# Capped attention before two expert layers: values in tiles of 32 columns in one piece with the sums, and the first two pairs' loads ahead of all others

## The chip, the cores and the metric

The kernel runs on one core of a Trainium2 chip. The core has a matrix engine (PE, whose weight loads the profile lists as PEld), three engines for element-wise work (DVE, ACT, POOL), and SP, which here issues nearly all DMAs. Each engine works through its own instructions in a fixed order and waits for the others by semaphores. The metric is the device time of one execution in microseconds (us), median of several.

## The reference

```
scores = q @ k.T / sqrt(64)                      # 2 x 12 heads, 448 x 448
scores = cap * tanh(scores / cap)                # cap = 30
attn = exp(scores - max); attn = attn / (sum(attn) + 1e-9)
x = attn @ v                                     # -> 896 tokens x 768
xn = x / rms(x) * rms_g
y = (silu(xn @ w_gate) * (xn @ w_val)) @ w_out   # 768 -> 1536 -> 768
a, b = y @ w1, y @ w2
out = ((a * b) @ w3) @ w_out2                    # 768 -> 1024 -> 1024 -> 768
```

All is float32. The maximum is not subtracted: tanh bounds the scores. The last two products have no nonlinearity between them, so the kernel multiplies w3 by w_out2 ahead, beside the attention.

## The kernel before

**Attention.** The 24 heads lie in 12 pairs, two heads to a pair, and two pairs make what is called a set here (`d` in the code, six sets). A set has seven groups of key chunks: six groups hold 128 keys of both heads of one pair, the two pairs taking turns, and the seventh holds the last 64 keys of all four heads. For a group `g`, `scores` (L406) multiplies on PE into a PSUM bank of ring `s`, which holds two groups; `tanh` (L425) and `exp` (L432) run over it on ACT and leave it in SBUF; `pv` (L438) multiplies by the values into `po`, 64 columns of the matrix for each head; and for every two groups `total` (L453) multiplies by ones into `pn`, 32 columns for each of the four heads, which gives the sums of the softmax. In this text S0 is the scores block of group 0, V0 its values block, N the sums of two groups. A float32 matmul shows as two passes, so a block of two matmuls is four rows (x4), and one of four is x8. When a set is through, its values are copied out (`take`), its sums inverted on DVE (`invert`, L486), spread by eight DMAs (`spread`, L497) and multiplied in (L505); squares are added up, and when the first or last six pairs are through, `normalize_x` makes the root mean square, scales (L322) and splits x into a high and a low half.

**Beside it.** `last_product` (L619) multiplies w3 by w_out2 in 64 items of three matmuls (L654 to L656), whose weights are unpacked by POOL, ACT and DVE (`weights`, L243). The items fill PE while the last set is inverted and normalised; then the first experts' products (L824 to L826) begin.

**Order.** All work is added to a planner (`Plan`, L55) as tasks with an engine, an estimated length and a rank. `order` (L89) plays the tasks through with these estimates, the ready task of lowest rank first, and the engines' instructions stand in the order that comes out. A task is one block on PE: scores, values and sums are tasks of their own (L541 to L553). Load tasks carry a rank that says how early SP issues them (`load_head` L387, `load_val` L402). The load of `cap` (L1115) is issued before the planner's work; it sets `tsc`, the scale that tanh reads.

Of the kernel before, what the change touches and what calls it, by code (L numbers as in the profile page):

```python
# [19 lines left out]
P = 128  # L20
B, H, S, D = 2, 12, 448, 64
# [5 lines left out]
CD = DM // P  # L27
# [4 lines left out]
KP = NK * P  # L32
NG = HP * 7 // 2
CQ = S // 4
CW = P // 4
# [19 lines left out]
class Plan:  # L55
# [19 lines left out]
    def add(self, engines, run, rank, after=(), makes=(), uses=(), size=0, behind=()):  # L75
        if not isinstance(engines, dict):
            engines = {engines[0]: engines[1]}
        i = len(self.tasks)
        for m in makes:
            self.bufs[m["tag"]].append((rank if m["first"] is None else m["first"], i, m))  # L80
        held = list(makes) + [u for u in uses if u is not None]
        for h in held:
            h["users"] += 1
        self.tasks.append(
            dict(on=engines, run=run, rank=rank, after=[x for x in after if x is not None], makes=list(makes), held=held, size=size, behind=list(behind))
        )
        return i
# [81 lines left out]
def body(ctx: ExitStack, tc, qk, v, cap, wgv, wdn, rg, w12, w3t, wo2, out):  # L169
# [44 lines left out]
    def layer(es, bounded):  # L214
# [145 lines left out]
        def attend():  # L360
# [26 lines left out]
            def load_head(p):  # L387
                def run(e, cols, new):
                    if new:
                        heads[p] = ring(ap, "qk", [P, S + KP])  # L390
                    e.dma_start(out=heads[p][:, cols], in_=qk[p][:, cols])

                when = first_of(p) - (7 if p == 0 else 5)
                cuts = [slice(0, S + P), slice(S + P, S + KP)] if p == 0 else [slice(0, S + KP)]
                h_done[p] = []
                for n, c in enumerate(cuts):
                    h_done[p].append(
                        add(("SP", 0.45), lambda e, c=c, n=n: run(e, c, n == 0), when + 0.1 * n, behind=h_done[p], makes=[] if n else [qkb[p]], uses=[qkb[p]] if n else [],
                            size=P * (c.stop - c.start) * 4)
                    )  # L400

            def load_val(p):  # L402
                def run(e):
                    vals[p] = ring(ap, "v", [P, 7, D])
                    e.dma_start(out=vals[p], in_=v[p])

                v_done[p] = add(("SP", 0.45), run, first_of(p) - 5.5 if p else -6.85, makes=[vb[p]], size=P * 7 * D * 4)

            def scores(g):
                def run(e):  # L410
                    chunks[g] = ring(ps, "s", [P, 2, 512], name="pss")
                    use = parts(g)
                    for j in range(2):
                        for p, c in use:

                            q = heads[p][j * D : (j + 1) * D]
                            if c < 3:
                                at, to, ks = j, slice(0, P), slice(S + c * P, S + (c + 1) * P)
                            else:
                                at, to, ks = p % 2, across(p, j), slice(S + 3 * P + j * D, S + 3 * P + (j + 1) * D)  # L420
                            e.matmul(chunks[g][to, at, :S], q[:, ks], q[:, :S], start=True, stop=True)  # L421

                return run

            def tanh(g):  # L425
                def run(e):
                    s = chunks[g]
                    chunks[g] = ring(ap, "t", [P, 2, S])
                    e.activation(chunks[g], s[:, :, :S], AF.Tanh, scale=tsc)  # L429

                return run

            def exp(g):
                def run(e):
                    e.activation(chunks[g], chunks[g], AF.Exp, scale=acap)  # L435

                return run

            def pv(g):


                def run(e):
                    for i in range(2):
                        for p, c in parts(g):
                            if c == 0 and i == 0:
                                pos[p] = ring(ps, "o", [P, 512], name="po")
                            rows, n = (slice(0, P), i) if c < 3 else (across(p, i), p % 2)
                            w = vals[p][rows, 2 * c + i if c < 3 else 6, :]
                            e.matmul(pos[p][i * D : (i + 1) * D, :S], w, chunks[g][rows, n, :], start=c == 0, stop=c == 3)  # L449

                return run

# [75 lines left out]
            for p in range(NP):  # L528
                load_head(p)
                load_val(p)  # L530
            exps, x_alloc, sq_last, pv_last, sum_last = {}, {}, {}, {}, {}
            every = []
            for g in range(NG):
                use = parts(g)
                sb = buf("s")
                qs = [qkb[p] for p, _ in use]
                need = []
                for p, c in use:
                    need += h_done[p][:1] if p == 0 and c == 0 else h_done[p]
                a = add(("PE", 0.83), scores(g), g - 2, after=need, makes=[sb], uses=qs)  # L540
                a = add(("ACT", 1.02), tanh(g), g, after=[a], makes=[tb[g]], uses=[sb])  # L541
                exps[g] = a = add(("ACT", 1.06), exp(g), g + 0.1, after=[a], uses=[tb[g]])
                c, last = use[0][1], use[-1][1] == 3
                a = add(("PE", 0.83), pv(g), g + 1, after=[exps[g]] + [v_done[p] for p, _ in use] + [pv_last.get(p) for p, _ in use],
                        makes=[ob[p] for p, c in use if c == 0], uses=[tb[g]] + [vb[p] for p, _ in use] + [ob[p] for p, c in use if c])
                for p, _ in use:
                    pv_last[p] = a
                if use[-1][0] % 2 == 0:
                    continue
                d = g // 7  # L550
                from_ = [g] if last else [g - 1, g]
                t = add(("PE", 0.83), total(d, c), g + 1.2, after=[exps[x] for x in from_] + [sum_last.get(d)], makes=[] if c else [nb[d]],
                        uses=[tb[x] for x in from_] + ([nb[d]] if c else []))  # L553
                sum_last[d] = t
                if not last:
                    continue
                r = g + 1.5
                b = 2 * d // (H // 2)
                taken = {}
                got = add(("DVE", 0.64), take_sum(d), r - 2, after=[t], makes=[smb[d]], uses=[nb[d]])  # L560
                for p in (2 * d, 2 * d + 1):
                    new = b not in x_alloc
                    taken[p] = add(dict(ACT=0.55, DVE=0.64), take(p), r - 2 + 0.1 * (p % 2), after=[a] + ([] if new else [x_alloc[b]]),
                                   makes=[xb[b]] if new else [], uses=[ob[p]] + ([] if new else [xb[b]]))
                    x_alloc.setdefault(b, taken[p])
                inv = [add(("DVE", 1.52), invert(d, c), r + 0.1 * c, after=[got], uses=[smb[d]]) for c in range(2)]
                for p in (2 * d, 2 * d + 1):
                    h = p % (H // 2)
                    sent = []
                    for i in range(4):  # L570
                        sent.append(add(("SP", 0.45), spread(p, i), r - 50, after=inv, behind=sent[-1:], makes=[] if i else [rbb[p]], uses=[smb[d]] + ([rbb[p]] if i else []), size=CW * S * 4))
                    a = add(("DVE", 0.66), normalize(p), r + 0.3, after=sent + [taken[p]], uses=[rbb[p], xb[b]])
                    every.append(a)
                    a = add(dict(DVE=0.66, POOL=1.3), square(p), r + 0.4, after=[a], makes=[sqb[p]] if h else [], uses=[xb[b]])
                    if h:
                        a = add(dict(DVE=0.66) if h == 5 else dict(DVE=0.66, POOL=1.3), add_square(p), r + 0.5, after=[a, sq_last[b]], uses=[sqb[p]])
                    sq_last[b] = a
                    every.append(a)
                    if p == NP // 2 + 1:
                        normalize_x(0, [sq_last[0]], g + 0.9)  # L580
# [531 lines left out]
                        add(("SP", 0.45), store(*done[1:]), -50, after=[done[0]], uses=[tmp[done[1]]], size=P * S * 4)  # L1112

        if bounded:
            nc.sync.dma_start(out=tsc, in_=cap.to_broadcast([P, 1]))  # L1115
            load_const()
            add(("SP", 0.45), lambda e: e.dma_start(out=rgt, in_=rg), -6.7, size=P * CD * 4)
            stored = last_product()
            over = attend()
        else:  # L1120
            attend_any()
            stored, over = [], []
# [62 lines left out]
```

## Time and profile before

| | |
|---|---|
| median of 3 runs | 624.87 us (624.56 to 625.26) |
| the profiled execution | 625.47 us, its span 623.3 us |
| PE busy | 608.6 us, 98% of the span |
| ACT, DVE, POOL busy | 265.7, 401.0, 141.6 us |
| attention on PE, first scores to last sums | 5.10 to 114.57 us |
| the first expert product | 145.68 us |

The span runs from the first to the last instruction of the profiled execution. The chain that ended last, 91% of it PE, says what each step waited for. A busy PE may still lose time: where the shape of the tiles in the matrix changes from one block to the next, a block takes longer, and this shows in how long the block stands in the chain, not as idle time.

### The profile page before, as it was taken

What the parts mean: (1) busy time and instruction counts of PE and PEld (TensorE: products, weight loads), DVE (VectorE), ACT (ScalarE), POOL (GpSimd) and SP (SyncE); (2) the same over time, 40 slices, a digit from 0 to 9 for tenths busy, and PEclk for the clock granted to TensorE, in tenths of its full rate; (3) what the DMA queues carried; (4) which work ended last, traced back from release to release, by engine and by line L of the source; (5) the groups of instructions that cost most, each with busy time, mean ns of one, the idle gap of its engine ahead of it and who ended that gap; (6) DMA issues with size and microseconds to landing.
All of it is one profiled execution on the core that took longest, in us unless ns stands there. A gap on an engine that the chain in (4) does not pass through costs nothing.

```text
span 623.3 us, 8065 instructions
## 1 busy us (share of the span) xinstructions
PE 608.6 (98%) x3088; PEld 490.6 (79%) x3088; DVE 401.0 (64%) x527; ACT 265.7 (43%) x359; POOL 141.6 (23%) x138
## 2 busy tenths in 40 slices
PE   5999999999999999999999999999999999999996
PEld 1222232798899999999999999999999999999995
DVE  2788685589866888435776555576657575627753
ACT  4988999156444343222334333333323343213220
POOL 3573200122343344211132222211122121000000
PEclk9999999999999999999999999999999999999999
DMA  8556421176455454218962323333331423105111
GB/s 309 214 177 209 148 60 42 54 238 203 146 197 167 169 193 148 68 67 255 331 217 102 101 102 103 102 110 121 119 108 50 152 90 97 35 0 151 56 49 64
DMA packets 32063, 82.93 MB, mean 133 GB/s; under 512 B 3728, under 2 KB 20752, under 8 KB 32016
## 3 DMA queue, kind: packets, MB, share of 16 engines
q1 hardware_dynamic: 32016, 82.33, 40.0%
q8 instruction: 26, 0.43, 0.3%
q14 instruction: 21, 0.17, 0.1%
HBM read 70.52 MB, written 9.04 MB: 128 GB/s over the span
## 4 chain that ended last, share of the span: by engine, by line
PE 91%; DMA 3%; DVE 2%; ACT 2%; issue 1%; SPq 0%; DVEq 0%; ACTq 0%
PE bank L826 22%; PE bank L825 22%; PE bank L824 22%; PE bank L1048 8%; PE pss L421 6%; PE po L449 6%; PE pn L463 3%; DMA wraw<-in_wgv 2%; DMA m_half<-mo 1%; DMA qk<-in_qk 1%; DVE whl L191 1%; DVE xraw L322 0%; ACT xn L184 0%; DVE sm L486 0%; ACT t L435 0%
## 5 line engine op out<-in xcount | busy, mean ns | idle before, releaser
L191 DVE TENSOR_TENSOR whl<-wraw,whl 128x768 fp32r<-128x768 f32 (+1 forms) x86 | 74.5, 867 | 69.5 <-POOL whl L188 58.5
L268 POOL TENSOR_SCALAR wraw<-wraw 128x768 int32<-128x768 uint32 (+1 forms) x68 | 76.0, 1118 | 152.9 <-DMA wraw<-in_w 57.8
L826 PE MATMUL bank<-xn,whl 128*128 128x448 f32 x288 | 105.8, 367 | 0.8 <-DVE whl L191 0.8
L824 PE MATMUL bank<-xn,whl 128*128 128x448 f32 x288 | 105.7, 367 | 0.3 <-ACT mo L184 0.3
L825 PE MATMUL bank<-xn,whl 128*128 128x448 f32 x288 | 105.6, 367 | 0.0
L272 DVE SCALAR_TENSOR_TENSOR wraw<-wraw 128x768 int32<-128x768 int32 (+1 forms) x76 | 71.4, 939 | 47.1 <-POOL wraw L268 47.1
L276 DVE SCALAR_TENSOR_TENSOR wraw<-wraw 128x768 int32<-128x768 int32 (+1 forms) x76 | 76.6, 1008 | 1.7
L188 POOL TENSOR_SCALAR whl<-wraw 128x768 fp32r<-128x768 f32 (+1 forms) x34 | 32.1, 943 | 196.4 <-PE bank L826 119.4
L184 ACT ACTIVATE whl<-wraw 128x768 fp32r<-128x768 f32 (+1 forms) x52 | 41.6, 801 | 73.8 <-PE bank L826 28.2
L824 PE MATMUL bank<-y,whl 128*128 128x448 f32 x192 | 70.7, 368 | 0.0
L825 PE MATMUL bank<-y,whl 128*128 128x448 f32 x192 | 70.7, 368 | 0.0
L826 PE MATMUL bank<-y,whl 128*128 128x448 f32 x192 | 70.7, 368 | 0.0
L259 ACT ACTIVATE wraw<-wraw 128x768 f32<-128x768 f32 (+1 forms) x54 | 47.5, 882 | 45.4 <-DMA wraw<-in_wgv 17.3
L826 PEld LDWEIGHTS bank<-xn,whl 128*128 128x128 f32 x288 | 54.1, 188 | 6.3 <-DVE whl L191 1.6
L824 PEld LDWEIGHTS bank<-xn,whl 128*128 128x128 f32 x288 | 54.1, 188 | 5.5 <-ACT mo L184 0.6
L825 PEld LDWEIGHTS bank<-xn,whl 128*128 128x128 f32 x288 | 54.1, 188 | 4.9
L824 PE MATMUL bank<-u,whl 128*128 128x448 f32 x144 | 52.8, 367 | 0.0
L826 PE MATMUL bank<-u,whl 128*128 128x448 f32 x144 | 52.8, 367 | 0.0
L825 PE MATMUL bank<-u,whl 128*128 128x448 f32 x144 | 52.8, 367 | 0.0
L421 PE MATMUL pss<-qk 64*128 64x448 f32 (+1 forms) x192 | 44.5, 604 | 5.1 <-DMA qk<-in_qk 5.1
L429 ACT ACTIVATE t<-pss,small 128x896 f32<-128x896 f32 x42 | 41.9, 998 | 10.7 <-PE pss L421 10.7
L435 ACT ACTIVATE t<-t,small 128x896 f32<-128x896 f32 x42 | 43.9, 1044 | 1.3
(99 smaller groups left out, 920.7 us busy)
## 6 DMA issues: line engine op xcount, KB each, us to landing
wraw<-in_wgv SPq DMA_DIRECT2D x24, 768.0 KB, 5.4
wraw<-in_w SPq DMA_DIRECT2D x16, 768.0 KB, 4.3
wraw<-in_wdn SPq DMA_DIRECT2D x12, 768.0 KB, 4.3
wraw<-in_w3t SPq DMA_DIRECT2D x16, 512.0 KB, 3.9
wraw<-in_wo SPq DMA_DIRECT2D x8, 768.0 KB, 6.6
qk<-in_qk SPq DMA_DIRECT2D x11, 480.0 KB, 4.5
m_half<-mo SPq DMA_DIRECT2D x16, 192.0 KB, 3.0
mo<-m_half SPq DMA_DIRECT2D x16, 192.0 KB, 5.1
```

Of the source, the lines that this page charges most:

```text
L191: e.tensor_tensor(lo, raw, r32(hi), op=ALU.subtract)
L259: e.activation(h, h, AF.Copy, scale=2.0**-112)
L268: e.tensor_scalar(l, l.bitcast(U32), 0.876 * 2.0**-29, 0.49, op0=ALU.mult, op1=ALU.add)
L272: e.scalar_tensor_tensor(l, h, 3, l, op0=ALU.logical_shift_left, op1=ALU.bitwise_or)
L276: e.scalar_tensor_tensor(l, h, -(2**31), l, op0=ALU.bitwise_and, op1=ALU.bitwise_or)
L421: e.matmul(chunks[g][to, at, :S], q[:, ks], q[:, :S], start=True, stop=True)
L429: e.activation(chunks[g], s[:, :, :S], AF.Tanh, scale=tsc)
L435: e.activation(chunks[g], chunks[g], AF.Exp, scale=acap)
L824: e.matmul(dst, whi[:, c, :], src(0, g, b), start=(g == 0), stop=False)
L825: e.matmul(dst, whi[:, c, :], src(1, g, b), start=False, stop=False)
L826: e.matmul(dst, wlo[:, c, :], src(0, g, b), start=False, stop=(g == total - 1))
L1048: e.matmul(st["bank", name], w[:, q, :], z_at(op, q, y), start=q == 0 and n == 0, stop=q == NQ - 1 and n == 2)
```

## The change

Values are multiplied in pieces of 32 columns (`CW`), the shape that the sums have, two matmuls for each head where one was. The values of two groups and their sums are one task on PE (`all_values`), which waits for both groups' exp; for the seventh group it is its values and sums. Scores could be put in one task by two (`two`), but the code has this off (`False and`). The queries and first 128 keys of the first two pairs are loaded first, then values and the other keys of both; `cap` is issued by ACT; `rg`, which is read at the end of attention, is issued later.

```diff
-                when = first_of(p) - (7 if p == 0 else 5)
-                cuts = [slice(0, S + P), slice(S + P, S + KP)] if p == 0 else [slice(0, S + KP)]
+                cuts = [slice(0, S + P), slice(S + P, S + KP)] if p < 2 else [slice(0, S + KP)]
+                whens = [(-8, -6.8), (-7.9, -6.7)][p] if p < 2 else [first_of(p) - 5]
...
-                v_done[p] = add(("SP", 0.45), run, first_of(p) - 5.5 if p else -6.85, makes=[vb[p]], size=P * 7 * D * 4)
+                v_done[p] = add(("SP", 0.45), run, first_of(p) - 5.5 if p > 1 else -6.85 + 0.1 * p, makes=[vb[p]], size=P * 7 * D * 4)
...
-                            w = vals[p][rows, 2 * c + i if c < 3 else 6, :]
-                            e.matmul(pos[p][i * D : (i + 1) * D, :S], w, chunks[g][rows, n, :], start=c == 0, stop=c == 3)
+                            for at in range(i * D, (i + 1) * D, CW):
+                                w = vals[p][rows, 2 * c + i if c < 3 else 6, at - i * D : at - i * D + CW]
+                                e.matmul(pos[p][at : at + CW, :S], w, chunks[g][rows, n, :], start=c == 0, stop=c == 3)
...
-                a = add(("PE", 0.83), scores(g), g - 2, after=need, makes=[sb], uses=qs)
-                a = add(("ACT", 1.02), tanh(g), g, after=[a], makes=[tb[g]], uses=[sb])
-                exps[g] = a = add(("ACT", 1.06), exp(g), g + 0.1, after=[a], uses=[tb[g]])
-                c, last = use[0][1], use[-1][1] == 3
-                a = add(("PE", 0.83), pv(g), g + 1, after=[exps[g]] + [v_done[p] for p, _ in use] + [pv_last.get(p) for p, _ in use],
-                        makes=[ob[p] for p, c in use if c == 0], uses=[tb[g]] + [vb[p] for p, _ in use] + [ob[p] for p, c in use if c])
...
+                two = False and use[0][1] < 3 and g > 1
+                if not two or use[0][0] % 2:
+                    of = [g - 1, g] if two else [g]
...
+                    a = add(("PE", 0.95 * len(of) - 0.18 * two), all_scores, of[0] - 2, after=[n for x in of for n in s_need[x][0]], makes=[s_need[x][1] for x in of], uses=[q for x in of for q in s_need[x][2]])
...
-                d = g // 7
-                from_ = [g] if last else [g - 1, g]
-                t = add(("PE", 0.83), total(d, c), g + 1.2, after=[exps[x] for x in from_] + [sum_last.get(d)], makes=[] if c else [nb[d]],
-                        uses=[tb[x] for x in from_] + ([nb[d]] if c else []))
-                sum_last[d] = t
+                c, last, d = use[0][1], use[-1][1] == 3, g // 7
+                of = [g] if last else [g - 1, g]
+
+                def all_values(e, of=of, d=d, c=c):
+                    for x in of:
+                        pv(x)(e)
+                    total(d, c)(e)
+
+                pair = (2 * d, 2 * d + 1)
+                banks_ = [ob[p] for p in pair] + [nb[d]]
+                a = add(("PE", 1.67 if last else 2.45), all_values, of[0] + 1, after=[exps[x] for x in of] + [v_done[p] for p in pair] + [sum_last.get(d)],
+                        makes=[] if c else banks_, uses=[tb[x] for x in of] + [vb[p] for p in pair] + (banks_ if c else []))
+                sum_last[d] = t = a
...
-            nc.sync.dma_start(out=tsc, in_=cap.to_broadcast([P, 1]))
+            nc.scalar.dma_start(out=tsc, in_=cap.to_broadcast([P, 1]))
             load_const()
-            add(("SP", 0.45), lambda e: e.dma_start(out=rgt, in_=rg), -6.7, size=P * CD * 4)
+            add(("SP", 0.45), lambda e: e.dma_start(out=rgt, in_=rg), 5.2, size=P * CD * 4)
```

The planner now puts the work in another order. On SP, the first DMAs of the program, before and now (`qk` holds a pair's queries and keys, `v` its values, `wraw` weights of w_out2):

```order
L1115 DMA small<-in_cap 128x1
L391 DMA qk<-in_qk 128x576
L391 DMA qk<-in_qk 128x384
L405 DMA v<-in_v 128x448
L1117 DMA small<-in_rg 128x6
L405 DMA v<-in_v 128x448
L391 DMA qk<-in_qk 128x960
L254 DMA wraw<-in_wo 128x1536 x3
```

```order
L391 DMA qk<-in_qk 128x576 x2
L406 DMA v<-in_v 128x448
L391 DMA qk<-in_qk 128x384
L406 DMA v<-in_v 128x448
L391 DMA qk<-in_qk 128x384
L254 DMA wraw<-in_wo 128x1536 x3
```

The first keys of pair 0 moved from second to first, those of pair 1 from seventh to second, and the first weights from eighth place to seventh.

On PE, the first blocks of the program, before and now (`pss` are scores, `po` values, `pn` sums; counts are matmuls, each of two passes):

```order
L421 MATMUL pss<-qk 128x448 x2
L449 MATMUL po<-t,v 64x448 x2
L421 MATMUL pss<-qk 128x448 x6
L449 MATMUL po<-t,v 64x448 x2
L463 MATMUL pn<-t,ones 32x448 x4
L421 MATMUL pss<-qk 128x448 x2
```

```order
L422 MATMUL pss<-qk 128x448 x8
L451 MATMUL po<-t,v 32x448 x8
L465 MATMUL pn<-t,ones 32x448 x4
L422 MATMUL pss<-qk 128x448 x4
L451 MATMUL po<-t,v 32x448 x8
L465 MATMUL pn<-t,ones 32x448 x4
L422 MATMUL pss<-qk 64x448 x4
```

Before, V0 stands behind S0, and values and sums stand apart; now S0 to S3 stand together, and each two groups' values stand with their sums. Over the attention the stretches of scores of 128 columns fall from 34 to 23 (those of the seventh groups, 64 columns, stay 6), the stretches of values from 41 to 24, and the 24 stretches of sums stand directly behind values of their own shape, where before they were stretches of their own; the stretches of items before the last sums rise from 6 to 9, with 12 items in them for 7, so that 52 stand behind the last sums for 57.

On ACT, between the seventh and the ninth group (`L436` is the exp, `L430` the tanh; before, nothing stood between them there), now:

```order
L436 ACTIVATE t<-t,small 128x896
L184 ACTIVATE wo<-wraw 128x768
L430 ACTIVATE t<-pss,small 128x896
L436 ACTIVATE t<-t,small 128x896
L430 ACTIVATE t<-pss,small 128x896
L184 ACTIVATE xraw<-po 128x448
L436 ACTIVATE t<-t,small 128x896
```

The high half of a weight chunk, which POOL made before, moved to ACT, and so did a copy of the first set's values.

## Rows read from the trace of the kernel before

**Rows 1.** The page's busy times of the whole span.

```profile
PE 608.6 (98%) x3088; PEld 490.6 (79%) x3088; DVE 401.0 (64%) x527; ACT 265.7 (43%) x359; POOL 141.6 (23%) x138
```

**Rows 2.** Waits of PE: engine line, waited for, us, times, longest.

```profile
PE pss L421 <- DMA qk<-in_qk: 5.1, 1, 5.1
PE po L449 <- ACT t L435: 2.2, 1, 2.2
PE bank L826 <- DVE whl L191: 0.8, 2, 0.6
PE bank L654 <- DVE mo L186: 0.4, 1, 0.4
PE bank L824 <- ACT mo L184: 0.3, 1, 0.3
```

**Rows 3.** Chain that ended last, first blocks: start, us, what.

```profile
0.74 0.40 SPq L1115
1.20 3.86 DMA qk<-in_qk
5.10 1.89 PE pss L421 x4
7.01 1.02 ACT t L429
8.05 1.05 ACT t L435
9.15 1.76 PE po L449 x4
```

**Rows 4.** The same chain, later blocks of attention and two items.

```profile
46.13 0.95 PE pss L421 x4
47.08 1.65 PE po L449 x8
49.69 0.89 PE pn L463 x8
50.58 0.90 PE po L449 x4
53.33 0.91 PE pss L421 x8
59.73 0.91 PE po L449 x8
84.56 0.37 PE bank L654
84.93 0.18 PE bank L655
```

**Rows 5.** The first ten us: stretch, busy of PE, PEld, DVE, ACT, POOL, clock, DMA, GB/s.

```profile
0.00:10.00 10.00, 2.72 (x8) 0.80 (x8) 0.95 (x8) 3.54 (x4) 0.45 (x6) 1.00 0.74 253
```

**Rows 6.** Timeline: start, us, engine, line, out<-in, idle before it.

```profile
4.90 0.15 DVE L209 TENSOR_SCALAR small<-small 128x1 f32<-128x1 f32 x1
14.90 0.97 PE L449 MATMUL po<-t,v 128*64 128x448 f32 x4
17.75 1.04 ACT L435 ACTIVATE t<-t,small 128x896 f32<-128x896 f32 x1
18.70 0.99 ACT L429 ACTIVATE t<-pss,small 128x896 f32<-128x896 f32 x1
19.72 1.05 ACT L435 ACTIVATE t<-t,small 128x896 f32<-128x896 f32 x1
...
22.60 0.97 DVE L276 SCALAR_TENSOR_TENSOR wraw<-wraw 128x768 int32<-128x768 int32 x1
```

**Rows 7.** Timeline behind the attention.

```profile
113.61 0.96 PE L463 MATMUL pn<-t,ones 64*32 64x448 f32 x8
...
135.80 4.27 DVE L322 SCALAR_TENSOR_TENSOR xraw<-xraw,small,acc 128x448 f32<-128x448 f32 x6
...
145.68 0.36 PE L824 MATMUL bank<-xn,whl 128*128 128x448 f32 x1
```

More of the change, by code (lines that the diff above doesn't have):

```diff
@@ L397, in load_head @@
                     h_done[p].append(
-                        add(("SP", 0.45), lambda e, c=c, n=n: run(e, c, n == 0), when + 0.1 * n, behind=h_done[p], makes=[] if n else [qkb[p]], uses=[qkb[p]] if n else [],
+                        add(("SP", 0.45), lambda e, c=c, n=n: run(e, c, n == 0), whens[n], behind=h_done[p], makes=[] if n else [qkb[p]], uses=[qkb[p]] if n else [],
                             size=P * (c.stop - c.start) * 4)
@@ L530, in attend @@
                 load_val(p)
-            exps, x_alloc, sq_last, pv_last, sum_last = {}, {}, {}, {}, {}
+            exps, x_alloc, sq_last, sum_last, s_need = {}, {}, {}, {}, []
             every = []
@@ L538, in attend @@
                 for p, c in use:
-                    need += h_done[p][:1] if p == 0 and c == 0 else h_done[p]
-                a = add(("PE", 0.83), scores(g), g - 2, after=need, makes=[sb], uses=qs)
-                a = add(("ACT", 1.02), tanh(g), g, after=[a], makes=[tb[g]], uses=[sb])
-                exps[g] = a = add(("ACT", 1.06), exp(g), g + 0.1, after=[a], uses=[tb[g]])
-                c, last = use[0][1], use[-1][1] == 3
-                a = add(("PE", 0.83), pv(g), g + 1, after=[exps[g]] + [v_done[p] for p, _ in use] + [pv_last.get(p) for p, _ in use],
-                        makes=[ob[p] for p, c in use if c == 0], uses=[tb[g]] + [vb[p] for p, _ in use] + [ob[p] for p, c in use if c])
@@ L546, in attend, with all_scores @@
-                for p, _ in use:
-                    pv_last[p] = a
+                    need += h_done[p][:1] if p < 2 and c == 0 else h_done[p]
+                s_need.append((need, sb, qs))
+                two = False and use[0][1] < 3 and g > 1
+                if not two or use[0][0] % 2:
+                    of = [g - 1, g] if two else [g]
+                    def all_scores(e, of=of):
+                        for x in of:
+                            scores(x)(e)
+                    a = add(("PE", 0.95 * len(of) - 0.18 * two), all_scores, of[0] - 2, after=[n for x in of for n in s_need[x][0]], makes=[s_need[x][1] for x in of], uses=[q for x in of for q in s_need[x][2]])
+                    tanhs = [add(("ACT", 1.02), tanh(x), of[0] + 0.05 * (x - of[0]) if two else g, after=[a], makes=[tb[x]], uses=[s_need[x][1]]) for x in of]
+                    for x, a in zip(of, tanhs):
+                        exps[x] = add(("ACT", 1.06), exp(x), x - (x - of[0]) * 0.95 + 0.1 if two else g + 0.1, after=[a], uses=[tb[x]])
@@ new lines, in all_values @@
+                def all_values(e, of=of, d=d, c=c):
+                    for x in of:
+                        pv(x)(e)
[4 more added lines that the diff above has]
+                        makes=[] if c else banks_, uses=[tb[x] for x in of] + [vb[p] for p in pair] + (banks_ if c else []))
```

## The prediction, made before the changed kernel was run

> **What bounds the kernel now.** The busy times come first: PE is busy for 608.6 of 623.3 us [rows 1], so a change counts by what it takes from PE's own time or from its few waits. Those are read next [rows 2]: 5.1 us for the first queries and keys, 2.2 us for the first exp, and 1.5 us in three later places, all of them behind the attention. Between 9.15 us and the last sums PE waits for nothing. So the attention is bound by PE, and the question is what its blocks are made of. The chain shows that [rows 4]: a scores block that follows another kind takes 0.95 us, a values block 0.90, a sums block 0.89; two values blocks that stand side by side take 1.65 together. The second costs 1.65 - 0.90 = 0.75 us. So streaming is 0.75 us a block, and every change of tile shape adds 0.20 us (scores), 0.15 (values), 0.14 (sums), 0.16 (the seventh group's scores, 0.91) or 0.19 (an item of the weight product, 0.37 for 0.18). That is the lever of this change. The start is the other place [rows 3]: S0 starts at 5.10, and until about 13 us blocks take twice their later time (1.89 for 0.95), as at 1.2 instead of 2.4 GHz, although the clock column reads 1.00 in this stretch [rows 5]; PE had not run before, and it stood still again between S0 and V0.
>
> **The change part by part.** *Fewer changes of shape.* Streaming stays: the same 42 scores, 42 values and 24 sums blocks, if four tiles of 32 columns run side by side as they do in the sums (four matmuls, eight passes, in 0.89 us, [rows 4]). The stretches behind a change of shape are counted in the orders. Scores: 34 to 23, 11 x 0.20 = 2.2 us. Values: 41 x 0.15 = 6.15 before, 24 x 0.14 = 3.36 now, since their tiles are now those of the sums; 2.8 us. Sums: 24 x 0.14 = 3.4 us gone, as no change stands ahead of them. Items: three stretches more, 3 x 0.19 = 0.6 us lost. Together 7.8 us, of which 0.2 lies in the first blocks and is counted there: 7.6 us.
>
> *The head.* SP issues the first queries at 0.74 instead of 1.20 [rows 3], so S0 starts near 4.64 and, at the lower clock, ends at 6.53. Pair 1's first part is 288 KB; at the 253 GB/s of the first ten us [rows 5] it lands 1.2 us later, at 5.8, in time. S1 needs no change of shape: 1.5 us at the lower clock, to 8.03. ACT: tanh 6.55 to 7.57, exp to 8.64 (1.02 and 1.05, [rows 3]), tanh of group 1 to 9.67, exp to 10.74. S2 runs from 8.03, S3 from 9.69 when its bank is read, and V0 starts at 10.75. Before, S0 to S3 and V0 were done at 14.90, where V1 starts [rows 6]; less V0 (0.90) that is 14.0. The head gives 14.0 - 10.75 = 3.25 us. From both sides: if the scores up to S3 all ran at the lower clock, V0 would start near 11.5 (2.5 us gained); if the queries land no earlier at all, 0.46 us of it goes. It cannot be much more than 3.25, since ACT's four activations in a row set it. `cap` on ACT costs ACT 0.4 us ahead of its table load, which hides behind the wait for S0; the scale was ready at 5.05 [rows 6] and has until 6.5. `rg` is moved past all early loads; it is read only when x is scaled, after half of the attention, so nothing is priced for it. The first weights go out 0.46 us earlier.
>
> *The new wait.* V0, V1 and N are now one piece that waits for the second exp, and PE's scores of the next groups stand behind it or ahead of it as the order has them. ACT needs 19.72 - 17.75 = 1.97 us for a group [rows 6], 3.95 for two; PE needs 0.95 + 0.75 + 0.14 + 3 x 0.75 = 4.1 us for two groups. PE is just the slower, so waits come only where ACT is behind. By hand, with these lengths: exp of groups 3 and 5 end at 14.7 and 18.7; the second piece waits for nothing, the third, ready at 18.15, waits 0.55. Behind the seventh group ACT has the high half of the third weight chunk, which needs a join that ended at 23.57 [rows 6], now some 0.46 earlier: ACT loses about 2 us with the activation itself, and PE waits 0.35, 1.25 and 0.55 in S9, S10 and the next piece. Later the exps of a piece are done before it is reached. One more wait stands in the fifth set: five items stand in a row there and change their bank after the second, and the copy on DVE that frees it stands behind the sums' reciprocals; I take 0.8 us. Sum 2.7 + 0.8 = 3.5 us lost. Bounds: none of it, or the third rival.
>
> *Behind the attention.* The last sums ended at 114.57, the first expert product began at 145.68 [rows 7], after 57 items. Now 52 items stand there: 52 x 0.52 + 0.95 = 28.0 us instead of 31.1. The five other items were done earlier, so this is no gain by itself, but the chain to the experts' x and weights must fit in 28.0. DVE scales x until 140.07, 25.5 us behind the last sums, and then, before, unpacked two chunks, so the low halves came at 145.3 and 146.4. In the new order the first chunk is unpacked ahead of the scaling and its low half stands right behind it: 25.5 + 0.95 = 26.5, which fits; the second, after three unpacking steps, a copy and its own 0.95, at 30.9, and is needed at 28.0 + 3.7 = 31.7. So nothing new waits, and of the 1.5 us of old waits [rows 2] I take half away: 0.75 us. Bounds: 0 and 1.5, if the chain keeps its length.
>
> The sum: 7.6 + 3.25 - 3.5 + 0.75 = 8.1 us. The profiled execution took 625.47 us, which makes 617.4; it stood 0.6 above the median of 624.87, so in the measure of the median 616.8. I say 616.7.
>
> *A rule that speaks against it.* In the seventh groups the two row halves of the matrix work at once on one bank: each head of a pair takes another row half, both write the pair's `po`. The row shows 0.91 us for all eight passes [rows 4], as for any block, and 0.96 for the sums of such a group [rows 7]. The Trainium skill, "TensorEngine Tiling (Array Packing)", Restrictions and Gotchas, says that different row tiles cannot access the same PSUM bank at the same time. By that rule the two halves would take turns, and such a block would need another 0.75 us; the row does not bear it out for tiles of 64 columns, and no run yet shows tiles of 64 rows by 32 columns, eight at a time.
>
> **The rivals.** *1. The end takes it back.* The chain behind the last sums keeps its 31.1 us, because SP's spreads, DVE's unpacking or a weight load set it and not the items. For it: DVE was the one waited for twice there [rows 2]. Against it: the new order unpacks one chunk earlier. The price is the 5 items (2.6 us) and the 0.75: 616.8 + 3.4 = 620.2.
>
> *2. No new wait.* ACT keeps ahead and the old waits vanish: 3.5 + 0.75 us more, 612.5. For it: ACT is busy for only 43% of the span [rows 1] and each wait is an estimate of a few tenths. Against it: the join on DVE is late in any case.
>
> *3. The slower side: pieces starve.* ACT has taken over copies and halves, its 3.95 us for two groups is 0.15 us from PE's 4.1, and every piece of values and sums needs the later of two exps. If not three but all 18 such pieces wait, the gain without these waits, 8.1 + 2.7 = 10.8 us, is gone from 0.60 us a piece on; at 0.9 us, which is the mean of the first three losses, 16.2 us are lost: 630. Against it: before, PE waited for no exp but the first [rows 2].
>
> *4. Small tiles do not overlap.* Eight tiles of 64 rows by 32 columns run four at a time: the six seventh groups take 0.75 us more each, 4.5 us: 621.3. For it: no row has eight tiles at once. This is also the time by the rule named above.
>
> **How the numbers follow.** Forecast 0.58, rival 1 0.15, rival 2 0.13, rival 3 0.06, rival 4 0.08. A measurement of this kernel tells a difference from 0.2%, that is 1.25 us. Forecast and rivals 1, 2 and 4 are all faster by more, with some 0.02 for mixtures of 1 and 4 that end within; of rival 3 0.05 is slower and 0.01 in between: faster 0.92, same 0.03, slower 0.05. The range goes from rival 2 to rival 4, 612.3 to 621.3, and leaves out rival 3 and tails.
>
> **What would show it.** Scores blocks side by side and the values in pieces of 2.24 + 0.14 us in the chain; 1.6 us for a seventh group's values and sums (2.4 would mean rival 4). V0 at 10.75 us or a few tenths from it. PE's waits for exp: some 2.7 us, all before 30 us; 10 us or more spread over the attention would be rival 3. The last sums at 109 to 110 us and the first expert product 28 us later; 31 would be rival 1. The prediction is wrong if the chain shows a change of shape between values and sums, or if the expert layers, which the change doesn't touch, move by more than a microsecond from the first product to the end.

## The result, and the profile after

The changed kernel took 619.77 us (median of 6 runs, 619.34 to 622.24), the kernel before 624.68 beside it (6 runs, 624.41 to 625.26): 0.9916 of the time, 95% interval 0.9902 to 0.9931. That is 4.9 us gained where 8.1 were forecast. The profiled execution took 619.81 us, its span 617.8 is 5.5 below that of before.

One execution of each kernel was traced, and in five of these fourteen (e1, e4, e8, e9, e12) the first half of the expert layers steps 0.207 us from matmul to matmul and not 0.202, some 2.4 us in all; so the experiments below are compared by the start of the first expert product in the traced execution, and the median times are given beside it (the traced executions of e3 and e7 lie 2.9 and 2.7 us below their medians).

The page's busy times, and its chain that ended last by engine:

```profile
PE 600.9 (97%) x3280; PEld 493.9 (80%) x3280; DVE 398.1 (64%) x522; ACT 266.4 (43%) x363; POOL 144.2 (23%) x139
...
PE 82%; DVE 6%; DMA 4%; SPq 3%; POOL 2%; issue 2%; ACT 0%; DVEq 0%; ACTq 0%; POOLq 0%
```

PE is busy for 7.7 us less [rows 1], and the chain has changed its nature: PE held 91% of it, now 82%. PE's waits up to 160 us (columns as in [rows 2]):

```profile
PE pss L422 <- DMA qk<-in_qk: 5.1, 1, 5.1
PE pss L422 <- ACT t L430: 2.3, 3, 0.9
PE pn L465 <- DVE sm L475: 1.7, 1, 1.7
PE bank L669 <- DVE mo L186: 1.0, 2, 0.7
PE bank L839 <- DVE mo L186: 0.6, 1, 0.6
PE bank L307 <- DVE acc L526: 0.3, 1, 0.3
```

Between 9.15 us and the last sums PE had waited for nothing. The chain itself (start, us, what), first where it is off PE, then where it is on it:

```profile
19.27 1.54 POOL wraw L268
20.84 0.97 DVE wraw L272
21.83 1.57 DVE wraw L276
23.43 0.92 ACT wo L184
...
53.05 3.42 DMA wraw<-in_w3t
56.61 1.12 POOL wraw L261
...
59.80 1.07 POOL wraw L268
60.90 0.74 DVE wraw L272
61.66 1.13 DVE wraw L276
62.80 0.61 DVE sm L475
...
94.43 0.91 PE po L451 x16
95.35 0.75 PE pn L465 x8
...
102.36 1.70 PE pss L422 x8
104.06 1.64 PE po L451 x16
105.71 0.75 PE pn L465 x8
```

The last rows answer to [rows 4] and are as forecast: two scores blocks 1.70, two groups' values 1.64 with sums of 0.75 behind them, 2.39 in all; the seventh group's values and sums 0.91 + 0.75. The upper rows are new: from 3.5 to 77 us the chain runs through the loads of weights, their unpacking on POOL and DVE, SP's spreads and the sums, not through PE. (Behind the last sums it is off PE in both kernels.) At 23.43 ACT makes the high half of a weight chunk that DVE has only just joined, and the tanh queued behind it is late; at 62.80 DVE takes the third set's sums out of their bank, late, because it stood behind joins that waited for POOL, and POOL for a DMA.

The head and the end, from the timeline (start, us, idle before in brackets), which answer to [rows 3, 6, 7]:

```profile
5.11 4.49 PE L422 MATMUL pss<-qk 64*128 64x448 f32 x12 [5.11 <-DMA qk<-in_qk]
7.02 1.01 ACT L430 ACTIVATE t<-pss,small 128x896 f32<-128x896 f32 x1 [0.99 <-PE pss L422]
10.05 1.02 PE L422 MATMUL pss<-qk 64*128 64x448 f32 x4 [0.45 <-ACT t L430]
11.00 1.71 PE L451 MATMUL po<-t,v 128*32 128x448 f32 x16
...
131.13 0.44 PE L669 MATMUL bank<-wo,whl 128*128 128x384 f32 x1 [0.32 <-DVE mo L186]
...
141.17 0.55 DVE L186 COPY mo<-bank 128x384 f32<-128x384 f32 x1
141.87 0.44 PE L839 MATMUL bank<-xn,whl 128*128 128x448 f32 x1 [0.58 <-DVE mo L186]
```

S0 starts at 5.11 as before, though its load went out 0.46 us earlier. The trace holds no record of the granted clock before 9.1 us, where blocks begin to take half their time, and in the kernel before none before 13.4 us; so the column's 1.00 [rows 5] says nothing of that stretch. The last sums end at 112.1 (114.5 before), the first product starts 29.8 us later.

To compare kernels, each stretch of PE from the first values block to the last sums is taken apart: streaming (0.75 us a block, 0.53 an item), changes (stretches times the prices of [rows 4]), and what is left, called lost:

```
                      first   stream-  changes  lost  last   items  first
                      values  ing                     sums   ahead  product
before                 9.15    84.7    18.2     2.4   114.5    7    145.7
changed               11.00    85.1    10.1     5.9   112.1   12    141.9
e1 64 columns         10.86    85.1    14.0     2.7   112.7   12    142.5
e2 apart               9.97    82.7    14.6     2.0   109.2    6    142.3
e3 loads of before    12.85    85.1    10.1     6.6   114.7   12    144.4
e4 cap behind pair 0  10.99    85.1    10.1     5.5   111.7   12    141.6
e5 two waits off      11.66    85.1    10.1     6.4   113.3   12    143.0
e6 e5, 64 columns     11.12    85.1    14.0     3.4   113.6   12    143.4
e7 e5, cap later      11.69    85.1    10.1     6.2   113.1   12    143.2
e8 loads alone         9.99    85.3    18.5     0.5   114.2   11    144.0
e9 own lanes          11.10    87.0     9.9     2.2   110.2   16    137.4
e10 e9, 64 columns    11.12    87.0    13.6     1.5   113.2   16    140.6
e11 changed again     11.37    85.1    10.1     5.2   111.8   12    141.9
e12 e9, apart         10.27    86.4    15.5     1.3   113.4   13    145.6
```

(Where the first values stand behind S0 alone, or ahead of S3, the scores that come later are in the streaming; the 2.4 lost of before are S1 to S3 and V0 at twice their later time. In e3 and e7, 1.6 of what is called lost is no wait: the granted clock falls there in the middle of the attention, as the last section shows.)

### The profile page after: what moved, and what is told of

It reads as the page before. It is cut to its first block, busy times and chain, and to the rows that moved or that the text cites. A ratio compares the mean times of both kernels' runs of the same rounds, so it can differ in the third digit from the quotient of the medians.

```text
span 617.8 us, 8451 instructions
## 1 busy us (share of the span) xinstructions
PE 600.9 (97%) x3280; PEld 493.9 (80%) x3280; DVE 398.1 (64%) x522; ACT 266.4 (43%) x363; POOL 144.2 (23%) x139
## 4 chain that ended last, share of the span: by engine, by line
PE 82%; DVE 6%; DMA 4%; SPq 3%; POOL 2%; issue 2%; ACT 0%; DVEq 0%; ACTq 0%; POOLq 0%
PE bank L839 23%; PE bank L841 23%; PE bank L840 22%; PE bank L1063 8%; SPq L499 3%; PE po L451 2%; DVE sm L488 2%; PE pss L422 1%; DMA m_half<-mo 1%; POOL wraw L261 1%; DMA wraw<-in_wo 1%; PE pn L465 1%; POOL wraw L268 1%; DVE wraw L272 1%; DMA rb<-sm 1%
## 5 line engine op out<-in xcount | busy, mean ns | idle before, releaser
L268 POOL TENSOR_SCALAR wraw<-wraw 128x768 int32<-128x768 uint32 (+1 forms) x68 | 79.1, 1164 | 136.9 <-DMA wraw<-in_w 54.2
L188 POOL TENSOR_SCALAR whl<-wraw 128x768 fp32r<-128x768 f32 (+1 forms) x34 | 30.6, 901 | 181.3 <-PE bank L841 122.4
L259 ACT ACTIVATE wraw<-wraw 128x768 f32<-128x768 f32 (+1 forms) x52 | 45.8, 882 | 45.6 <-DMA wraw<-in_wgv 16.0
L422 PE MATMUL pss<-qk 64*128 64x448 f32 (+1 forms) x192 | 41.9, 594 | 7.4 <-DMA qk<-in_qk 5.1
L436 ACT ACTIVATE t<-t,small 128x896 f32<-128x896 f32 x42 | 43.8, 1043 | 1.3
L430 ACT ACTIVATE t<-pss,small 128x896 f32<-128x896 f32 x42 | 41.8, 995 | 5.7 <-PE pss L422 5.5
```

The costliest lines, as they stand in the source:

```text
L259: e.activation(h, h, AF.Copy, scale=2.0**-112)
L268: e.tensor_scalar(l, l.bitcast(U32), 0.876 * 2.0**-29, 0.49, op0=ALU.mult, op1=ALU.add)
```

## The experiments

**e1: values in 64 columns, all else as changed.**

```diff
-for at in range(i * D, (i + 1) * D, CW):
-    e.matmul(pos[p][at : at + CW, :S], w, ...)
+e.matmul(pos[p][i * D : (i + 1) * D, :S], w, ...)
```

> The changed kernel with the values multiplied in tiles of 64 columns again, still in one piece with the sums; the order on every engine is that of the changed kernel. Theory (the tile shape carries the gain): 24 changes of shape between values and sums come back at 0.14 us each, 3.4 us, so the last sums end at 115.5 instead of 112.1 and the time is 623.2; sums behind values stand 0.89 us again. Rival (the one piece and fewer scores stretches carry it, not the columns): no more than 0.5 us, 619.8 to 620.3.

Measured: 621.05 us, 0.9926 of before (0.9898 to 0.9955). The changes are there, 3.9 us of them, but last sums and first product are 0.6 us later only. PE's waits show why:

```profile
PE pss L422 <- ACT t L430: 1.4, 3, 0.9
...
PE bank L838 <- DVE mo L186: 1.0, 1, 1.0
```

The wait for the third set's sums is gone: PE, slower, comes when they have been taken. The time lies between theory and rival, and neither had this reason; 3.2 of the 3.9 us that the shape saves are waited away in the changed kernel.

**e2: 32 columns, but scores, values and sums as tasks of their own** (the lines of before in place of `all_values`).

> The changed kernel with scores, values and sums as tasks of their own again, in tiles of 32 columns. The order then has 33 stretches of 128-column scores for 23, 42 stretches of values and sums for 22, 6 of items for 8. Theory (each change of shape costs 0.14 to 0.20 us wherever it stands): 10 x 0.20 + 20 x 0.14 - 2 x 0.19 = 4.4 us more in changes; the waits of PE for a late exp or a late sum, 5.4 us over the attention of the changed kernel, may fall to as little as nothing, since a block waits for one exp and not two: 618.8 to 624.2, and I say 622.5, with the waits of attention at 3 to 4 us. Rival (the waits come from ACT and DVE being late and not from the one piece): the waits stay above 5 us, 624.

Measured: 620.48 us, 0.9923 (0.9894 to 0.9953). Changes 4.5 us more than in the changed kernel, lost 3.9 less: first product 142.3 for 141.9. The lost time fell below the theory's 3 to 4; the rival is out as it was put (late engines and not the one piece). It does not show that the piece alone makes the waits: the 4.5 us more of changes also give ACT and DVE time, and e9 keeps the piece and loses 2.2 only. The one piece had gained next to nothing here.

**e3: the loads of before in the changed kernel.**

> The changed kernel with the loads of the kernel before: cap first on SP, then pair 0, pair 1's first keys seventh. Theory (the head is worth what the traces show, V0 at 11.0 for 14.0): 3.0 us of the gain go, 622.8; the first piece of values starts near 14. Rival (the later waits eat it: ACT, DVE and the weights are as late as before in either order, so a later start only shortens waits): 619.8 to 621, with the waits of the first set below 1 us instead of 2.3.

Measured: 624.93 us, 0.9986 (0.9967 to 1.0005); first values 1.85 us later, first product 2.5. The time missed both theory and rival. The waits of the first set fall to 0.7 as the rival had it, but 3.7 are lost in the second set: 2.0 are a wait, which ends when DVE has taken the sums (45.33) and copied the values (45.92) behind a weight's join and low half, and 1.6 come behind it, where the granted clock is 0.50 for 3.4 us. So the loads are worth about 2.5 us here, 1.6 of them by way of the clock; e8, without such a fall, gives 2.4.

**e4: cap on SP behind the first queries; e7: cap behind the first keys of both pairs, on top of e5.**

```diff
-nc.scalar.dma_start(out=tsc, in_=cap.to_broadcast([P, 1]))
+cap_in = add(("SP", 0.45), lambda e: e.dma_start(out=tsc, ...), -7.95, size=P * 4)    # e7: -7.85
+scale = add(("DVE", 0.6), lambda e: scale_const(), -20, after=[cap_in])    # every tanh now waits for scale
```

> The changed kernel with cap loaded by SP right behind the first queries, and not by ACT beside them; the order on PE, DVE and POOL is the same. In both kernels S0 started at 5.1, though its load was issued 0.46 us earlier in the changed one, and the transfers ran at 100 to 200 GB/s from 2.4 to 4.8 us. Theory (the 128 packets of 4 bytes of cap hold up the queries, on the same queue or on another): the queries land 1 us earlier or more, S0 starts at 4.1 or before, and the time falls by 0.5 to 1.5 us, to 618.3 to 619.3. Rival (the first transfer of an execution is late by itself): S0 at 5.1, cap later, tanh not before 7, 619.8 or more.

> The kernel of e5_free with cap loaded by SP behind the first keys of both pairs. With cap between them the queries landed at 3.67 for 5.11, but the second pair's keys only at 6.2, and the first values block stood at 10.99 as before. Theory (the 128 small packets of cap hold up whatever is behind or beside them): S0 at 3.7, S1 by 5.5, tanh at 6.0 to 6.5, first values at 10.3 to 10.6, and the first product 0.4 to 0.7 us earlier than in e5. Rival (ACT waits for cap now): tanh at 7.0 or later, nothing gained.

Measured: e4 620.96 us, 0.9931 (0.9904 to 0.9958); e7 624.42, 0.9984 (0.9964 to 1.0004). The timeline of e4:

```profile
3.67 1.86 PE L424 MATMUL pss<-qk 64*128 64x448 f32 x4 [3.67 <-DMA qk<-in_qk]
6.21 4.85 PE L424 MATMUL pss<-qk 64*128 64x448 f32 x12 [0.68 <-DMA qk<-in_qk]
10.99 1.81 PE L453 MATMUL po<-t,v 128*32 128x448 f32 x16
```

and of e7:

```profile
3.70 3.36 PE L424 MATMUL pss<-qk 64*128 64x448 f32 x8 [3.70 <-DMA qk<-in_qk]
6.87 1.01 ACT L432 ACTIVATE t<-pss,small 128x896 f32<-128x896 f32 x1 [0.36 <-DVE small L214]
7.92 3.83 PE L424 MATMUL pss<-qk 64*128 64x448 f32 x8 [0.87 <-ACT t L432]
11.69 1.20 PE L453 MATMUL po<-t,v 128*32 128x448 f32 x8
```

The theory of the transfer holds: with cap's 128 packets of 4 bytes behind them the queries land 1.4 us earlier, and whatever cap stands ahead of is late (in e4 the second pair's keys, 6.2). So S0 stayed at 5.1 because of cap, which stood ahead of the queries before and ran beside them on the other queue in the changed kernel, and not because a first transfer is slow. But no time comes of it: in e4 S1 is late, in e7 the scale is, PE stands 0.87 us, and S2 and S3 take 3.83 us, twice their later time (the record of the granted clock begins at 12.2 us in this trace). Both theories missed that last part. Later in e7, at 53 us, the clock falls as in e3, 1.6 of its 6.2 us lost.

**e5: the two large waits taken away one by one; e6: the same with 64 columns.** (The cuts of e5 and e9 are shortened.)

```diff
-a = add(unary, first, rank + 0.5, ...)                       # third chunk of w_out2
+a = add(dict(POOL=1.02), first, rank + 0.5, ...)
-got = add(("DVE", 0.64), take_sum(d), ...)
+got = add(("ACT", 0.55) if d == 2 else ("DVE", 0.64), take_sum(d), ...)
```

> The changed kernel without its two largest waits inside the attention: the high half of the third chunk of w_out2 is made by POOL, not by ACT, and the third set's sums are taken out of their bank by ACT, not by DVE. The order on PE is the same. Theory (these waits have given back the gain of the fewer changes of shape): PE's lost time after 23 us (2.3) and after 60 us (1.9) falls below 0.5 each, the last sums end at 108 to 109 instead of 112.1, and the first expert product starts at 138.5 to 139.5 instead of 141.9; time 616 to 617. Rival (ACT is late by itself, and the wait only moves to the next block or to the end): last sums not before 111, first product at 141 or later, 619.

> The kernel of e5_free (third chunk's high half on POOL, third set's sums taken by ACT) with values in tiles of 64 columns, as in e1_cols64. In e1 the changes of shape cost 3.9 us more than in the changed kernel, but the last sums ended only 0.6 later, since 3.2 us of waits were gone. Theory (the shape is worth its 24 x 0.14 to 0.16 us as soon as nothing waits): last sums and first product 3 to 4 us later than in e5. Rival (another limit stands close behind, ACT's 1.97 us a group or DVE): 1 us or less.

Measured: e5 621.93 us, 0.9958 (0.9936 to 0.9981); e6 622.02, 0.9955 (0.9941 to 0.9968). My theory fell: 6.4 us lost in e5, and the rival's signs (last sums not before 111, first product at 141 or later) came. The waits, and DVE's timeline where the largest of them ends, in e5:

```profile
PE po L451 <- DVE xraw L186: 2.4, 1, 2.4
PE pss L422 <- ACT t L430: 2.1, 3, 1.0
```

```profile
58.63 0.70 DVE L272 SCALAR_TENSOR_TENSOR wraw<-wraw 128x512 int32<-128x512 int32 x1 [1.33 <-POOL wraw L268]
...
60.95 0.69 DVE L272 SCALAR_TENSOR_TENSOR wraw<-wraw 128x512 int32<-128x512 int32 x1 [0.55 <-POOL wraw L268]
61.68 1.02 DVE L276 SCALAR_TENSOR_TENSOR wraw<-wraw 128x512 int32<-128x512 int32 x1
62.62 0.61 DVE L186 COPY xraw<-po 128x448 f32<-128x448 f32 x1
```

The planner gave the copy of the values, which ACT had done, to DVE, and there it stands behind the same joins. On ACT another high half waits 2.68 us for its join at 46 us. And e6 is again only 0.4 us behind e5. That suggests one cause and not two places: weights' steps, late, ahead of attention's steps on ACT and DVE. e9 tests it.

**e8: the new loads alone, on the kernel before.**

> The kernel before with nothing but the new loads: first keys of both pairs in front, cap on ACT's queue, rg later; values in 64 columns, tasks apart. The order on PE then runs S0 to S2 together. Theory (head and shape add up): the head alone gives 2.5 to 3 us, last sums 2.5 to 3 earlier than before with the same work ahead of them, first product at 142.7 to 143.2, 622; and e2_apart32, the same but for 32 columns (and a planner's length of 0.95 for the scores), is another 2 to 3 us ahead of it in attention. Rival (with an earlier start this kernel too runs into ACT and DVE): waits of 1.5 us or more appear in the first set, first product at 144 or later.

Measured: 623.69 us, 0.9977 (0.9967 to 0.9986). Last sums 0.3 us earlier with four items (2.1 us) more ahead of them: 2.4 us, near the theory; nothing new waits in the attention (0.5). The first product, at 144.0, came where the rival had it, but by a wait of 0.9 for a weight's high half just ahead of it, not by the rival's waits in the first set; two waits behind it cost 1.6. Beside e2, which differs by the 32 columns and a planner's length, the columns save 3.9 us of changes, and 1.5 of them are lost in waits.

**e9: in the attention ACT unpacks no weights, and ACT alone takes sums and values out of their banks (DVE keeps the joins, the reciprocals and the scaling); e10: the same with 64 columns; e11: the changed kernel again, on the same chip.**

```diff
-unary = dict(POOL=0.25 + N / 1000, ACT=0.2 + N / 1200)
+unary = dict(POOL=0.25 + N / 1000) if rank < 2000 else dict(POOL=..., ACT=...)
-got = add(("DVE", 0.64), take_sum(d), ...)
+got = add(("ACT", 0.55), take_sum(d), ...)
-taken[p] = add(dict(ACT=0.55, DVE=0.64), take(p), ...)
+taken[p] = add(("ACT", 0.55), take(p), ...)
```

> The changed kernel, but in the attention ACT does no unpacking of weights (POOL does it), and ACT alone takes sums and values out of their banks, so that neither tanh and exp nor a bank stands behind a step that waits for weights. In e5_free the two waits were taken away one by one and came back elsewhere: 2.4 us for a bank whose copy stood on DVE behind joins that waited for weights, 2.1 us for a tanh behind a high half on ACT. Theory (what PE waits for is weights' steps standing ahead of attention's on ACT and DVE): PE's lost time between the first values and the last sums falls from 5.9 to 2 or less; with 16 items ahead of the last sums for 12, these end at 108 to 110.5 and the first product starts at 137 to 139.5, 4.5 to 2.4 earlier: 615.3 to 617.4. Rival (ACT's own work is the bound: 7 x 1.97 + 3 x 0.5 = 15.3 us a set, and PE has 7 x (0.75 + 0.75) + 4 x 0.75 + some 1.7 for changes = 15.2): waits stay at 4 us or more, spread over the sets, and the time stays at 619 to 620.

> The kernel of e9_own_lanes with values in tiles of 64 columns in the same pieces; the order on every engine is that of e9. Theory (the shape's worth shows where nothing waits): 24 x 0.16 = 3.9 us more in changes, and 3 to 4 us later at the last sums and the first product than e9; time 3 us above e9. Rival (ACT or DVE set the pace): 1 us or less, as in e1 against the changed kernel (0.6) and e6 against e5 (0.4).

> The changed kernel once more, as it is, beside e9 and e10 on one chip. If its time and its waits are those of its first profile: 619.3 to 620.3, last sums at 112, 2.3 us lost after 23 us and 1.9 after 60. If the waits depend on how soon weights land in an execution, they stand in other places with a sum of 4 to 7 us, and the time differs by 0.5 us or more.

Measured: e9 618.74 us, 0.9897 (0.9867 to 0.9927); e10 620.52, 0.9929 (0.9904 to 0.9954); e11 620.73, 0.9931 (0.9908 to 0.9953). The chain of e9 by engine, from its page:

```profile
PE 89%; DVE 4%; ACT 2%; DMA 2%; SPq 2%; issue 1%; DVEq 0%
```

and PE's waits in e9:

```profile
PE pss L422 <- ACT t L430: 1.9, 2, 1.1
PE bank L841 <- DVE whl L191: 1.4, 1, 1.4
PE bank L669 <- ACT mo L184: 1.1, 1, 1.1
```

The theory holds by the trace, its rival (ACT's own work) is out: lost 2.2 for 5.9 (2 or less was expected; 5.2 in e11), PE back at 89% of the chain, first product at 137.4, 4.5 us ahead of e11. More items stand ahead of the last sums, 16 for 12, and fill PE; but the first product stands behind all 64 in both, so its 4.5 us do not come of that. And now the shape shows its worth: e10 has 3.7 us more in changes, its last sums are 3.0 later, its first product 3.2, its time 1.8. e9 is the fastest by the first product, but 1.6 us go in one wait behind it (a low half on DVE, at 149 us; 1.4 of them idle). Its time missed the expected 615.3 to 617.4, and the intervals of e9 and e11 overlap: that e9 beats the changed kernel in time, by 2.0 us of the medians, is likely and not shown. e11 repeats the changed kernel's waits in the same places, 5.2 us in sum.

**e12: e9 with scores, values and sums apart.**

> The kernel of e9_own_lanes with scores, values and sums as tasks of their own, in tiles of 32 columns. The order then has 43 stretches of values and sums for 23, 33 of scores for 22, 10 of items for 7, and 13 items ahead of the last sums for 16. Theory (with no waits in the way, the one piece is worth its changes): 20 x 0.14 + 11 x 0.20 + 3 x 0.19 = 5.6 us more in changes, less some 1 us of waits behind the second exp that a piece has and a single block has not: first product at 141.5 to 142.5 for 137.4, time 3.5 to 5 us above e9. Rival (the piece's waits are as large as what it saves): first product within 1.5 us of e9.

Measured: 626.05 us, 1.0007 (0.9997 to 1.0018). Changes 5.6 us more, as counted, lost 0.9 less. The last sums are 3.3 us later with three items (1.6) fewer ahead: in the attention the one piece is worth some 4.8 us where little else waits. The first product came at 145.6 and not at 142, since its bank's copy on ACT stood behind the halves of x: a wait of 4.5 us that belongs to the end, not to the piece.

## Why the prediction was right in direction and too large

Term by term, profiled execution against profiled execution (forecast, then trace):

- *Fewer changes of shape*, 7.6: 7.7. From V1 before, and from V0 now, 17.8 us of changes became 10.1. e1, e6 and e10 give 3.7 to 3.9 for the columns, e12 5.6 for the one piece.
- *The head*, 3.25: 3.15. V1 stood at 14.90 [rows 6]; now V0, which streams 0.75, starts at 11.00. The way there differs: S0 did not come at 4.64, so ACT's four activations ran from 7.02 to about 11.0 and not from 6.55 to 10.74, and V0 came 0.25 late. The value moves between executions with the place where the clock rises: the first record of the granted clock stands at 9.1 us here, at 10.9 in e11 and at 11.3 in e5, and V0 at 11.00, 11.37 and 11.66.
- *The new wait*, -3.5: -5.8 (the 5.9 lost, less 0.1 lost behind V1 before). **This is the step that failed.** Of its parts, S9, S10 and the piece behind were set at 2.15 and cost 2.35, the bank in the fifth set 0.8 and cost 0.9; the third piece's 0.55 did not come. What I had not seen is the third set's sums, 1.9 us, and four small ones of 0.12 to 0.17. The text said that later the exps of a piece are done before it is reached; that is so. But, one bank of items apart, I looked for PE's waits in ACT's tanh and exp alone, and the largest single one came from a bank of the attention, which DVE frees, behind weights.
- *The end*, 0.75: 0.4. The five items that moved ahead delay the last sums by 2.6 and were to shorten the end by as much; it shortened by 1.4. Two copies of items on DVE freed their banks late, at 131.13 and 141.87. Behind the first product the old waits of DVE's low halves and ACT's copy [rows 2] went, 1.1 us of idle and 1.6 of time, where I took 0.75: from the first product to the end the span takes 476.0 us for 477.6. The prediction named a move of more than one microsecond there as a sign of being wrong, and this one came.

The sum: 7.7 + 3.15 - 5.8 - 2.6 + 1.4 + 1.6 = 5.45 us of span (5.5 measured), for 8.1. Three terms missed, by -2.3, -1.2 and +0.85; the last, in the forecast's favour, hides a quarter of the other two. Rival 1 came in part: the end took 29.8 us, between 28.0 and 31.1, and took back 1.2 of the 2.6. Rival 2 fails. Rival 3 named the right kind of thing, pieces that starve, and the wrong place: no piece waited for an exp. Rival 4 fails: 64-row tiles of 32 columns run eight at a time, 0.91 and 0.75 us for 16 and 8 passes. The rule of the Trainium skill, "TensorEngine Tiling (Array Packing)", Restrictions and Gotchas, that different row tiles cannot access one bank at the same time, is not borne out by this time.

The common point was in the forecast and not followed: ACT's two groups, 3.95 us by [rows 6], lie just below PE's 4.1 in the changed kernel. Before, the changes of shape (18.2 us over 42 groups) gave the other engines that much time to be late in; with 10.1 a late step on another engine shows at once, as e1 shows from the other side (3.9 us more of changes, 3.2 less lost). The planner put these steps there by its estimates; how far those were off was not measured. e9 shows the cause by taking it away; e5 shows that taking away single waits does not.

## What to carry to other kernels

When the busiest engine is made faster, count first what the others feed it in the same time: here 7.7 us of work were saved and 2.3 more than expected were waited away, by steps of which one at least was no later than before (the join that ended at 23.57 [rows 6] now ends at 23.4). On an engine that works in order, keep the steps that free a bank or feed the busiest engine away from steps that wait for transfers; moving single ones only moved the wait in e5. And test the worth of a change once with the waits out of the way: 64 for 32 columns cost 0.6 us in the changed kernel and 3.2 in e9.

## What the runs showed of the chip

In three executions the clock fell in mid-kernel, each time in or behind waits of PE. By windows (stretch, busy of PE, PEld, DVE, ACT, POOL, granted clock, DMA, GB/s), first e12, behind its wait of 4.5 us:

```profile
141.00:146.00 5.00, 0.47 (x2) 0.40 (x2) 4.97 (x6) 4.64 (x10) 2.60 (x3) 0.78 0.49 175
146.00:151.00 5.00, 5.00 (x15) 4.42 (x15) 5.00 (x7) 1.16 (x1) 0.88 (x1) 0.54 0.35 100
151.00:156.00 5.00, 5.00 (x27) 4.53 (x25) 2.37 (x4) 2.27 (x3) 1.05 (x2) 1.00 1.02 389
```

The granted clock is 0.78 in the window of the wait and 0.54 in the 5 us behind it, about the lower of its two levels (1.2 of 2.4 GHz), and the matmuls step 0.37 us apart there instead of 0.207: 13 steps take 4.99 us for 2.76, 2.2 us on top of the wait. In e3, behind a wait of 2.0 us, and in e7, behind two waits of 0.65 and 0.98 with a scores block between them, the window is shorter (one line each, then a block in it):

```profile
46.60:50.00 3.40, 3.37 (x18) 0.91 (x20) 3.40 (x4) 0.49 (x1) 1.87 (x3) 0.50 0.76 276
48.10 1.75 PE L465 MATMUL pn<-t,ones 128*32 128x448 f32 x8
```

```profile
53.20:56.60 3.40, 3.40 (x18) 0.79 (x20) 2.11 (x5) 3.33 (x5) 0.00 (x0) 0.50 0.71 227
53.71 3.12 PE L453 MATMUL po<-t,v 128*32 128x448 f32 x16
```

The block of sums in e3 takes 1.75 us where others show 0.94, the two groups' values in e7 3.12 where others show 1.71. Set against the usual steps from block to block, each fall costs 1.6 us. The wait of 2.4 us in e5 and that of 1.7 in the changed kernel were not followed by one.
